# Transposing k and q on VectorE, norms from a diagonal, and a rebuilt join in a fused delta-rule and mixer kernel

## The chip, the cores and the metric

The kernel runs on one core of a Trainium2 chip. The time is device time in microseconds, the median of five runs. TensorE multiplies matrices into PSUM; VectorE and ScalarE do elementwise work; GpSimd ("POOL") sets up constants and issues the weight loads; SyncE ("SP") issues most other transfers. Each engine takes its own instructions strictly in the order of the program. All data is float32.

## The reference, cut to what matters

```python
B, H, S, D = 4, 8, 768, 48
k_n = k / (np.linalg.norm(k, axis=-1, keepdims=True) + 1e-06)
for t in range(S):
    y[:, :, t] = q_t @ state                       # per batch and head, D x D state
    v_old = k_t @ state
    state = state + beta_t * outer(k_t, v_t - v_old)   # k_t is a row of k_n
x = y as (B, S, H * D)                             # d_model = 384
h = x^T @ U @ V                                    # rank 32, over the sequence
u = x + h^T
out = u + relu(u @ w_ch1) @ w_ch2                  # hidden 1536
```

The weights arrive as 64-bit floats and are converted on the chip.

## The kernel before, in words

**Units.** The sequence of each batch is cut into chunks of 64 tokens, 12 a batch; six chunks of all eight heads are a *unit*, so there are eight units, two for each batch. For each unit the kernel needs k and q with the head dimension on the partitions, the products K K^T (`pg`) and K Q^T (`qk`), and the inverse of a triangular 64x64 matrix for each head and chunk (`zt`), which turns the token-by-token recurrence into one step for each chunk.

**Turning k and q (L516 to L535).** k is loaded with tokens on partitions (`kn`), q into `qn`. For each pair of chunks `turn` does four 128x128 transposes on TensorE (`p_t`), and ScalarE copies the result to `kq`. A unit has 24 of them. `products` then forms 16 small products for each pair (`p_g`).

**Norms and c (L443 to L514, L240).** Squares of k, a reduction on VectorE (L464), roots on ScalarE, and, with beta (transposed at the start by `p_bt`, L245), c = beta / norm^2. c changes layout by a transpose `p_ct` (L493) and a round trip through DRAM (`scrc`, `cp`, L499 and L505). v is scaled by the norm (L511).

**Inverse (`blocks`, L602).** `pg`'s 32x32 diagonal blocks go through DRAM (`scr`, L624) to `gs`, where each of 96 partitions holds one block; after a multiplication by c (L652), pairs of VectorE operations (L668, L674) do the substitution in `xt`. The result goes back through DRAM (`scr2`, L683) to `zt` and `zc`. Units 0 and 1 invert 16x16 blocks (15 pairs of operations) and put them together in `join` (L774), a chain of small TensorE products (`p_e`, `p_d`, `p_x`, `p_v`) with evacuations between; it runs in three thirds. Later units invert 32x32 blocks (31 pairs) and need only `p_x` and `p_v` (L722, L736).

**Recurrence (`recur`, L866).** For each chunk: `p_y` from the state, `rhs` (VectorE), `p_s`, `z` (ScalarE), the state's update `p_s` and the output `p_y`, `s` (VectorE). The mixer of a batch follows: `front` (`p_tt`, `p_h`, `p_u`) and `wide` (`p_f` and `p_o`, 36 + 36 matmuls of 128x128x384 for each half of a batch).

**Weights (`load_weights`, L282).** GpSimd loads slices of 768 KB into two alternating buffers (`wide`, `stage`), and five VectorE operations and one ScalarE operation convert each. Parts of w2's place are used early for other tiles (`early`, L218).

**The order.** Nothing is scheduled at run time. Each part is a Python generator; `run` (L140) keeps an estimated clock for each engine and always emits the step that could start first, with a place number as priority. So a changed part moves the order of all engines. On SP every transfer stands in one queue, and of its transfers at most eight are under way: each waits for the one that was issued eight before it. `gate` (L368) makes GpSimd wait for a value before it issues later loads.

## Time and profile before

| | us |
|---|---|
| median of five runs (676.03 to 679.97) | 678.88 |
| profiled execution, its own time | 678.88 |
| its span | 677.1 |
| first p_s of batch 0 starts | 59.81 |
| last p_y of batch 0 starts | 128.81 |
| first p_f starts | 150.34 |

A row of the profile names the line, the engine and the operation, the output and inputs, and the shape. "x8" counts instructions; a float32 matmul counts as two passes, a transpose as one. "Idle before" is the time the engine waited ahead of the instruction and what released it. The span is cut into 40 slices of 16.9 us in the page's second part; its digits are tenths of busy time, and PEclk is the granted TensorE clock in tenths. The busy time by stage gives us of each engine in a stretch of time.

### The profile page before, as it was taken

How to read it: one execution, taken by the hardware profiler on the slowest of the kernel's cores; microseconds unless marked ns; L12 is line 12 of the kernel's file. 1: busy time of each engine (PE TensorE's matmuls, PEld its weight loads, DVE VectorE, ACT ScalarE, POOL GpSimd, SP SyncE). 2: the span in 40 equal slices, each digit the busy share in tenths (PEclk: the TensorE clock that was granted, in tenths of full speed). 3: DMA queues.
4: the chain of work that ended last, by engine and by line, in shares of the span. 5: the costliest groups of instructions: out<-in, count | busy, mean ns of one | idle time of the engine just before them, and what ended most of it. 6: DMA issues, size and time to landing. Idle time of an engine off the chain costs nothing.

```text
span 677.1 us, 19682 instructions
## 1 busy us (share of the span) xinstructions
PE 623.3 (92%) x8676; PEld 399.7 (59%) x8676; DVE 318.1 (47%) x795; ACT 199.1 (29%) x487; POOL 43.3 (6%) x84
## 2 busy tenths in 40 slices
PE   5538799769999999989999999999999999999997
PEld 4437688536555666546556655665655555555554
DVE  6666688578888124871942187368111111000000
ACT  2406456424221352144314422422321221120210
POOL 6451000100100000000000000000000000000000
PEclk9856555759999999999999999999999999999999
DMA  8585747742721332246133321420300000000000
GB/s 123 115 194 151 152 115 188 169 79 35 185 53 37 69 66 60 48 84 122 22 68 64 69 54 45 76 61 2 60 14 26 1 1 24 12 1 23 13 10 24
DMA packets 143892, 46.00 MB, mean 68 GB/s; under 512 B 136960, under 2 KB 140032, under 8 KB 143808
## 3 DMA queue, kind: packets, MB, share of 16 engines
q1 hardware_dynamic: 133952, 30.99, 22.8%
q0 software_dynamic: 3552, 12.88, 6.7%
q10 hardware_dynamic: 6304, 0.89, 0.8%
q8 instruction: 68, 1.11, 0.7%
q14 instruction: 16, 0.13, 0.1%
HBM read 33.62 MB, written 11.11 MB: 66 GB/s over the span
## 4 chain that ended last, share of the span: by engine, by line
PE 81%; DVE 7%; DMA 6%; ACT 2%; SPq 2%; issue 1%; ACTq 1%; DVEq 0%
PE p_o L1058 28%; PE p_f L1038 27%; PE p_y L870 4%; PE p_g L553 3%; PE p_t L529 3%; PE p_s L921 2%; PE p_s L907 2%; DMA scr<-xt 2%; PE p_y L929 2%; DVE xt L674 2%; DVE prod L668 2%; PE p_u L1005 1%; PE p_h L995 1%; PE p_e L794 1%; DMA zt<-scr 1%
## 5 line engine op out<-in xcount | busy, mean ns | idle before, releaser
L1038 PE MATMUL p_f<-ut,w_sb 128*128 128x384 f32 x576 | 204.3, 500 | 0.2 <-ACT h_f L1023 0.2
L1058 PE MATMUL p_o<-w_sb,h_f 128*128 128x384 f32 x576 | 201.1, 495 | 0.0
L1038 PEld LDWEIGHTS p_f<-ut,w_sb 128*128 128x128 f32 x576 | 105.1, 191 | 65.2 <-issue 1.8
L1058 PEld LDWEIGHTS p_o<-w_sb,h_f 128*128 128x128 f32 x576 | 104.6, 190 | 63.4
L1023 ACT ACTIVATE h_f<-p_f 128x384 f32<-128x384 f32 x96 | 47.1, 491 | 205.8 <-PE p_f L1038 205.8
L1028 DVE TENSOR_TENSOR x<-x,p_o 128x384 f32<-128x384 f32 x24 | 13.2, 553 | 130.5 <-PE p_o L1058 130.5
L674 DVE TENSOR_TENSOR xt<-xt,prod 96x112 f32<-96x112 f32 (+21 forms) x216 | 70.5, 326 | 7.4
L668 DVE TENSOR_TENSOR prod<-gs,xt 96x112 f32<-96x112 f32 (+21 forms) x216 | 70.0, 324 | 6.2
L553 PE MATMUL p_g<-kq 48*64 48x64 f32 x1536 | 39.8, 250 | 9.7 <-DVE qk L569 8.2
L944 DVE TENSOR_TENSOR s<-s,p_s 128x192 f32<-128x192 f32 x40 | 14.1, 352 | 69.0 <-PE p_s L921 64.1
L553 PEld LDWEIGHTS p_g<-kq 48*64 48x64 f32 x1536 | 33.4, 159 | 18.6 <-DVE qk L569 7.7
L951 ACT COPY x<-p_y 64x192 f32<-64x192 f32 x96 | 30.0, 313 | 39.2 <-PE p_y L929 34.1
L870 PEld LDWEIGHTS p_y<-s,kq 48*64 48x64 f32 x1408 | 28.4, 149 | 19.6 <-issue 10.9
L535 ACT COPY kq<-p_t 128x512 f32<-128x512 f32 x48 | 27.4, 587 | 38.8 <-PE p_t L529 38.6
L916 ACT COPY z<-p_s 128x192 f32<-128x192 f32 x48 | 15.3, 318 | 73.6 <-PE p_s L907 73.4
L900 DVE TENSOR_TENSOR rhs<-vn,p_y 128x192 f32<-128x192 f32 x44 | 15.5, 351 | 41.2 <-PE p_y L870 40.8
L870 PE MATMUL p_y<-s,kq 48*64 48x48 f32 x1408 | 33.9, 237 | 0.8 <-DVE s L944 0.6
L907 PEld LDWEIGHTS p_s<-rhs,zt 64*64 64x64 f32 x704 | 16.1, 146 | 22.0 <-issue 17.7
L921 PEld LDWEIGHTS p_s<-z,kn 64*64 64x64 f32 x704 | 16.0, 148 | 19.4 <-issue 16.5
L907 PE MATMUL p_s<-rhs,zt 64*64 64x48 f32 x704 | 21.7, 240 | 3.5 <-DVE qk L569 1.7
L794 PE MATMUL p_e<-zt,pg 64*64 64x32 f32 x192 | 12.0, 291 | 13.1 <-DMA zt<-scr 11.9
L637 POOL MEMSET xt<- 96x1056 f32 x6 | 5.9, 978 | 278.8 <-DMA scr<-xt 278.8
(122 smaller groups left out, 530.3 us busy)
## 6 DMA issues: line engine op xcount, KB each, us to landing
wide<-in_moe_w_ch_dram POOLq DMA_DIRECT2D x6, 768.0 KB, 5.3
stage<-in_moe_w_ch_dram POOLq DMA_DIRECT2D x6, 768.0 KB, 5.8
out_dram<-x SPq DMA_DIRECT2D x24, 192.0 KB, 2.1
kn<-in_k_dram SPq DMA_DIRECT2D x60, 72.0 KB, 3.0
qn<-in_q_dram SPq DMA_DIRECT2D x48, 72.0 KB, 3.1
vn<-in_v_dram SPq DMA_DIRECT2D x48, 72.0 KB, 2.5
gs<-scr SPq DMA_DIRECT2D x8, 384.0 KB, 4.0
scr<-xt SPq DMA_DIRECT2D x8, 384.0 KB, 4.5
```

The costliest lines, as they stand in the source:

```text
L529: nc.tensor.transpose(p_t[:, x, j], t[:, c, 2 * j : 2 * j + 2].rearrange("p s d -> p (s d)"), ident,)
L535: nc.scalar.copy(places, p_t)
L553: nc.tensor.matmul(p_g[par][to, c, j], kq[rows, c0 + c, j, 0, cols], kq[rows, c0 + c, j, i, cols], start=True, stop=True,)
L668: nc.vector.tensor_tensor(out=prod, in0=gb[:, :, j : j + 1, j + 1 :].to_broadcast([NP, split, m, w]), in1=xb[:, :, 0:m, j : j + 1].to_broa ...
L674: nc.vector.tensor_tensor(out=xb[:, :, 0:m, j + 1 :], in0=xb[:, :, 0:m, j + 1 :], in1=prod, op=ALU.subtract,)
L870: nc.tensor.matmul(p[half(x ^ par), par, D * (2 * i + j) : D * (2 * i + j) + D], kq[half(par, D), cu, j, i, half(x)], s_old[half(par, D), ...
L907: nc.tensor.matmul(p_s[half(x), par, D * (2 + j) : D * (2 + j) + D], zt[half(x ^ par), cu, par, j], rhs[half(x ^ par), 2 * j + par], start ...
L921: nc.tensor.matmul(p_s[half(par), x, D * j : D * j + D], kn[half(x), cu, 2 * j + par], z[half(x), 2 * j + par], start=True, stop=True,)
L951: nc.scalar.copy(tokens_of(b, c, g), pair_of(p_y, 1)[half(g)])
L1023: nc.scalar.activation(hs[f], p_f, ACTF.Relu)
L1038: nc.tensor.matmul(p_f, w1_sb[:, t, f * 128 : (f + 1) * 128], ut[:, t], start=(t == 0), stop=(t == KT - 1),)
L1058: nc.tensor.matmul(p_os[c], hs[e][:, c * 128 : c * 128 + 128], w2_sb[:, e], start=(e == 0), stop=(e == FT - 1),)
```

## The change

- **k and q, units 2 to 7.** `turn_all` loads them in pieces of 32 tokens by 32 or 16 dimensions straight from DRAM into `qn`, used as a staging tile, with 16 transfers each on SP, and one VectorE transpose of 128x1536 in blocks of 32x32 (L481) writes the turned k or q. `kq` becomes two tiles, `kt` and `qt`. Units 0 and 1 keep TensorE. k is still loaded in its own layout for the recurrence.
- **Norms and c.** The diagonal of K K^T is in `gs` already; its root is the norm. `norm` and c are computed there (four VectorE operations on 96x32), in the layout that the inverse uses; four small matmuls (`p_n`) bring the norm to token layout for v. Beta is loaded in the blocks' layout, four transfers a unit on SP. Squares, reduction, `p_bt`, `p_ct` and c's round trip are gone.
- **Join.** `p_e` and `p_d` work on 32x32 tiles. The blocks for `zt` are no longer loaded but copied from `zc` by ScalarE (`blocks_of_32`), behind `xz`; `zc` is loaded on two queues for unit 0. One VectorE subtraction replaces eight ScalarE and four VectorE pieces.
- **Weights and order.** Odd slices of w2 are staged in w2's own last part; the U and V loads come first on GpSimd; q and v of unit 0 and the first w1 slice wait for unit 0's inverse (`gate(0)`), q and v of unit 1 and later slices for its `zc` (`gate(1)`). Batch 1's recurrence waits for w1's slices, no longer for w2's. The copy of `pg` for units 0 and 1 is shared by ScalarE and VectorE.

In the order that results, SP issues the 16 transfers of unit 2's q ahead of its scr, and on TensorE unit 2's `p_n` stands ahead of batch 0's `p_tt`.

```diff
+    def load_beta(n):
+        b, hf = divmod(n, 2)
+        if n > 1:
+            yield need(("scr", n - 1))
+        yield step(sp=2.1, then=2.5)
+        for i in range(4):
+            g, a = divmod(i, 2)
+            nc.sync.dma_start(
+                out=betas[CS * i : CS * i + CS, n],
+                in_=beta[b, 4 * g : 4 * g + 4, hf * UC * L : (hf + 1) * UC * L].rearrange(
+                    "s (c a t) -> c s a t", c=UC, a=2
+                )[:, :, a],
+            )
...
-            if i % 2:
+            if i in (W2 + 1, W2 + 3):
+                at = WIDE * (2 + (i - W2 + 1) // 2)
+                wide = early[:, at : at + 2 * n].bitcast(I32)
...
-                yield need(("weights", i - 2), *[("v", 0)] * (i == 1), *[("opened", 1)] * (i == 2))
+                last = i - 2 if i < W2 + 5 else i - 1
+                yield need(("weights", last))
+                if i > 1:
+                    yield need(("opened", i > 3))
...
+    def turn_all(n):
+        b, hf = divmod(n, 2)
+        stage = qn.rearrange("p c s d -> p (c s d)")
+        places = stage.rearrange("p (x j m d) -> p x j m d", x=2, j=2, d=BK)
+        yield need(("queries turned", n - 1))
+        for i, (name, src) in enumerate((("keys", k), ("queries", q))):
+            for par in range(2):
+                for half_d in range(2):
+                    rows = slice(L * par + BK * half_d, L * par + BK * half_d + BK)
+                    ds = slice(BK * half_d, min(D, BK * half_d + BK))
+                    for x in range(2):
+                        yield step(sp=1.2)
+                        for j in range(2):
+                            h = 4 * (x ^ par) + 2 * j + par
+                            nc.sync.dma_start(
+                                out=places[rows, x, j, :, 0 : ds.stop - ds.start],
+                                in_=src[b, h, hf * UC * L : (hf + 1) * UC * L, ds].rearrange(
+                                    "(m t) d -> t m d", t=BK
+                                ),
+                            )
+            emitted((name, n), 8.0)
+            yield need((name, n), ("room", n))
+            yield step(dve=1.8)
+            nc.vector.transpose(made[n][0][i].rearrange("p x j c t -> p (x j c t)"), stage)
+            emitted((name + " turned", n), 0.1)
...
         def key_pair(c0):
-            yield from turn([(kn, c0), (kn, c0 + 1)], kq[:, c0 : c0 + 2, :, 0])
+            if n < 2:
+                yield from turn([(kn, c0), (kn, c0 + 1)], kq[0][:, :, :, c0 : c0 + 2])
             yield from products(c0, 0)
...
-        yield need(("c", n), ("inverted", n - 1))
+        yield need(("inverted", n - 1), ("beta", n))
+        norm = small.tile([NP, BK], FP32, name="norm")
+        yield step(act=0.25, then=0.1)
+        nc.scalar.sqrt(norm, gs.rearrange("p i j -> p (i j)")[:, 0 : BK * BK : BK + 1])
+        yield step(dve=0.9, then=0.1)
+        nc.vector.tensor_scalar_add(norm, norm, 1e-6)
+        cp = small.tile([NP, BK], FP32, name="cp")
+        nc.vector.reciprocal(cp, norm)
+        cb = small.tile([NP, BK], FP32, name="cb")
+        nc.vector.tensor_tensor(out=cb, in0=cp, in1=betas[:, n], op=ALU.mult)
+        nc.vector.tensor_tensor(out=cp, in0=cp, in1=cb, op=ALU.mult)
+        def norms():
+            yield step(pe=0.25, then=0.1, take=("one",))
+            p_n = ps_one([128, CS], "p_n")
+            for i in range(4):
+                nc.tensor.matmul(
+                    p_n[BK * i : BK * i + BK], norm, ident[0:NP, CS * i : CS * i + CS],
+                    start=True, stop=True,
+                )
...
-            nc.sync.dma_start(out=zc[BK * i : BK * i + BK], in_=blk[i])
+            two[i % 2].dma_start(out=zc[BK * i : BK * i + BK], in_=blk[i])
...
-        for i in range(4):
-            (nc.scalar if n == 0 else nc.sync).dma_start(out=diagonal(zt, i), in_=blk[i])
...
+                nc.tensor.matmul(
+                    p_e[rows, e], pg[rows, c, j, r, at], zc[rows, e, SB:BK],
+                    start=True, stop=True,
+                )
...
-            nc.scalar.mul(diagonal(zt, i)[0:SB, qs, SB:BK], of, -1.0)
-            if a == 0:
-                nc.vector.tensor_scalar_mul(zc[BK * i : BK * i + SB, :, SB:BK], of, -1.0)
+        nc.vector.tensor_tensor(
+            out=zc[:, :, SB:BK], in0=zc[:, :, SB:BK], in1=p_d, op=ALU.subtract
+        )
+        def blocks_of_32():
+            yield step(act=1.5)
+            for i in range(4):
+                nc.scalar.copy(diagonal(zt, i)[:, qs], zc[quarter[i]])
+            emitted(("diagonal", n, third), 0.1)
```

## The prediction

> **What bounds the kernel now.** I read the page first, then the busy time by stage, then the timelines of TensorE, VectorE and SP, because the page's shares mix two very different stages.
>
> ```profile
> PE 623.3 (92%) x8676; PEld 399.7 (59%) x8676; DVE 318.1 (47%) x795; ACT 199.1 (29%) x487; POOL 43.3 (6%) x84
> PE   5538799769999999989999999999999999999997
> PEclk9856555759999999999999999999999999999999
> ```
>
> From slice 10 on TensorE is full at full clock; before it, TensorE has gaps and is granted about half its clock. The busy time by stage (us; PE, PEld, DVE, ACT and POOL busy, granted clock, DMA share, GB/s) says the same with numbers:
>
> ```profile
> 0.00:40.00 40.00, 22.16 (x346) 18.37 (x346) 27.12 (x72) 11.19 (x27) 23.67 (x56) 0.86 0.75 140
> 60.00:80.00 20.00, 15.05 (x412) 13.14 (x412) 12.94 (x26) 10.69 (x30) 1.12 (x2) 0.59 0.77 177
> 80.00:100.00 20.00, 19.02 (x540) 17.69 (x544) 15.54 (x29) 10.69 (x27) 1.06 (x2) 0.50 0.42 110
> 300.00:400.00 100.00, 99.48 (x1664) 62.07 (x1665) 46.62 (x127) 33.86 (x83) 1.95 (x2) 1.00 0.36 71
> ```
>
> So there are two sums: a chain of latencies up to the first wide product p_f (150.34 us), and a TensorE total from there to 677.1, 526.8 us, in which a TensorE instruction that goes is time that goes. The timeline of TensorE has the points on which the first sum hangs (start, duration, instruction, idle before it):
>
> ```profile
> 47.40 3.59 PE L794 MATMUL p_e<-zt,pg 64*64 64x32 f32 x62 [1.58 <-DMA zt<-scr]
> 59.81 0.75 PE L907 MATMUL p_s<-vn,zt 64*64 64x48 f32 x16
> 70.85 0.39 PE L794 MATMUL p_e<-zt,pg 64*64 64x32 f32 x2 [3.24 <-DMA zt<-scr]
> 116.16 1.92 PE L529 MATMUL p_t<-ident,w_sb 128*128 128x128 f32 x8
> 139.86 1.65 PE L980 MATMUL p_tt<-tt,quarters 128*128 128x384 f32 x2 [5.72 <-DVE tt L977]
> 150.34 4.21 PE L1038 MATMUL p_f<-ut,w_sb 128*128 128x384 f32 x6
> ```
>
> The 5.72 us in front of the second p_tt are VectorE's, which sat behind the blocks of unit 2, as its timeline shows:
>
> ```profile
> 134.73 1.22 DVE L652 TENSOR_TENSOR gs<-gs,cp 96x1024 f32<-96x1024 f32 x1 [6.55 <-DMA gs<-scr]
> ```
>
> **The change, part by part. (a) Up to the inverse of unit 0.** The chain of waits has p_bt (12.40, 2.69 us) between the second and third key product. It goes; the first two pairs' products now stand together, so the third is 9.23 + 2.1 (two products) + 1.05 (p_t) + 0.7 (copy) + 1.1 = 14.2 instead of 16.2, and its evacuation is split over ScalarE and VectorE (0.4): scr leaves at 14.7 instead of 17.01. By the same intervals as before (gs issued 3.8 later, landed 4.0 later by its median) gs is there at 22.5. Before, the multiply at 25.91 waited for cp, the round trip of c through DRAM, which goes. In its place stand, after gs, one small square root (0.2, like L474), four small VectorE operations (0.17+0.30+0.18+0.18, L478 to L483), and a 0.4 us copy of unit 1 that the order puts ahead: 24.1. Gain 1.8. U's and V's conversion stand ahead of these on VectorE; POOL, which no longer issues q first (5.17 us), sends V by about 9 us, so I price that wait at 0; if V were late, the gain here is gone.
>
> **(b) Inverse to first recurrence.** The 30 operations are the same. scr2 takes 5.67 us with vn, V and q in flight; gated, it meets q, a w1 slice and vn, as much: 0 (the bounds are -2.5, as unit 1's scr2 took 3.37, and +1.5). Then zt (4 transfers on ScalarE's queue, last issue 43.26, landed 47.26) goes, and zc's four are split over two queues: 1.1 issue and 4.0 to land instead of 6.4. Gain 1.2. The join, from 47.40 to p_s at 59.81, is 12.4. p_e and p_d become twice as many 32x32 tiles with 16 columns; the nearest row is p_v of L736 (96 passes in 1.02 at full clock, so about 21 ns at half), 64 passes in 1.35 per third against 1.8 and 1.0 before: level. What shortens it is that the eight ScalarE and four VectorE pieces of p_d (0.27 and 0.28 each, taking turns) become one subtraction of 128x128 (0.3) and the transposition (0.43), and that p_x reads zc itself. Step by step: p_e two thirds 2.7, p_d 1.4 after a 0.35 scale, 0.75 on VectorE, p_x 1.0, xz 0.7, four new zt copies of 32x256 (0.37 each, ahead of the last scale on ScalarE) 1.5, zt 0.75, hops: 9.7. Gain 2.7. First p_s: 59.8 - 5.7 = 54.1.
>
> **(c) Recurrence of batch 0, 69.5 us to 129.3.** Unit 1's inverse no longer queues so long behind the joins; its scr2 goes at about 53 (58.68 before) and only zc must land (SP's zt was 2.2 later than zc): of the 4.3 us without work before 71.91 I take 2.3 off. The transposes p_t of unit 2 (1.11+1.92+0.66+0.66+0.65 = 5.0) go: 4.0, as they are only nearly always in the way. VectorE gets two transposes of 128x1536. It does 128x256 in 425 ns and 128x384 in 574, so 1.16 ns a column: about 1.9 us each; one falls ahead of a state update. Against it the reduction (1.35) and four norm operations (0.83) go: 0. [...] The trace grants 0.50 from 80 to 100 us with TensorE 95% busy. [...] I go by the row. Recurrence: 6.3 less, ends near 117.3.
>
> **(d) From there to p_f.** Now SP's queue decides. Behind unit 0's last use (kn goes at 95.70 before, 87.7 now) stand 8 transfers of k (5.8), 8 of v (6.5), **16 of q at 0.55 (8.8)** and only then scr<-pg of unit 2: about 109. Before, gs was issued 7.5 after it and landed 5.4 later: 122 now, 134.64 before. TensorE stands behind it too: p_n (norm of unit 2) is ahead of p_tt. From gs: root 0.3, VectorE 0.95, p_n 0.4, one p_g 0.6 to 1.1, p_tt 2.8, copy 0.6, two p_g 2.2, p_tt 1.65, copy 0.6, then 7.5 as before (8.2 less a p_t and p_g): 17.5, so p_f at 139.5. Of the 12 us won, 10.8 arrive.
>
> **(e) The TensorE-bound rest, 526.8 us.** p_t:
>
> ```profile
> 192.00:300.00 108.00, 4.94 (x32) 1.00 0.28 59
> 300.00:420.00 120.00, 6.01 (x40) 1.00 0.30 61
> 420.00:565.00 145.00, 3.66 (x24) 1.00 0.15 32
> 257.83 1.02 PE p_t L529 x8
> ```
>
> (The first three are p_t's busy time by stage, the last a piece of the chain.) Busy times overlap; the chain has 1.02 for 8, so 96 transposes are 12.2, and 20 of unit 3 after 150 (1.09+1.04+0.66) 2.8. p_n and p_ct (0.29+0.2) give way to four small matmuls (0.3): 1.0 for five units. ScalarE's evacuations (0.59 each) were hidden, nothing. In exchange SP issues 24 more transfers a unit. Their cost is in when they land:
>
> ```profile
> kn<-in_k_dram SPq DMA_DIRECT2D x60, 72.0 KB, 3.0
> zc<-scr SPq DMA_DIRECT2D x24, 48.0 KB, 2.1
> ```
>
> A load of k has 384 pieces of 192 B; the new ones 384 of 128 or 64 B, like zc's. [...] By the rows, though, such a transfer is issued every 0.55 us and lands in 2 to 4, so 16 of them need 12 and a pair of halves with its 1.9 us transposes 28, against some 60 us per unit, with SP's other 24 transfers and waits about 20. By the row the cost is 0. [...] The join of unit 2 is covered too: its inverse starts near 133 and ends near 157, 16 transfers of unit 3's q may stand ahead of its scr2, and its blocks land near 170, while the order brings TensorE to p_x only after 36 p_f, 12 p_o and the products, about 41 us after p_f starts (180). The same 36 p_f (26 us) hide the conversion of w2, staged in w2's own last part: 0, and what a slice is late if that cover is gone. The four beta loads a unit (0.5 each on SP) and the changed order of zt's blocks cost nothing here. What I charge is VectorE's 1.9 us ahead of a rhs or state update: three products of 0.35 us (2.1 with their weights) usually cover it, so 2 in all (bounds -2.5, as TensorE waited twice for the 1.26 us reduction in the chain, and 8 x 1.9 = 15). Sum: 526.8 - 12.2 - 2.8 - 1.0 + 2 = 512.8.
>
> **Sum.** 139.5 + 512.8 = 652.3 of span. The profiled run was 678.88 with a span of 677.1, 1.8 around it, and 678.88 is also the median of the five, so no correction: 654.1.
>
> **Rivals.** (1) The start gains nothing: SP's 16 transfers, or the diagonal's wait for gs, take the place of what went. For it: gs already ended VectorE's longest wait, and (d) leans on an SP order. Against: zt, cp and p_bt are certainly gone. Then 677.1 - 14.0 + 1.8 = 665. (2) Slower: VectorE blocks at the head of its queue. L481 waits for all 16 loads, and behind it stand the rhs and state updates that feed TensorE, which is in order too. Place: units 4 to 7, after 190 us. SP also has outputs in that queue that wait for VectorE (207.5 us of waits on L1028), so loads can start late. With a gain of 25, eight transposes must each be late by 3.1 us beyond their cover for no change; at 5 us each 15 us are lost: 694 at worst, 686 as its middle. Against: DMA share is 0.36 or less there. [...]
>
> **How the numbers follow.** Forecast 0.52 (646 to 661); start gains nothing 0.20 (661 to 673); slower 0.10; more 0.18 (632 to 646). Leaving out a tenth at each end gives 638 to 675. About 0.3% (2 us) is what a measurement of this kernel tells from no change; 677 to 681 is nearly empty between (1) and (2): 0.02. Faster 0.88, slower 0.10.
>
> **What would show it.** Right: scr<-pg of unit 0 near 14.7, first p_s near 54, gs of unit 2 near 122 with p_n and p_tt directly behind it, p_f near 139, p_t at 72 instead of 192, L481 near 1.9 us, and from p_f to the end about 513. Wrong: waits of L481 on qn's loads, gaps on TensorE after 190, or a p_e of unit 1 that still waits 4 us.

## The result, and the profile after

The changed kernel takes 673.74 us (median of 43 runs, 668.24 to 683.01) against 678.97 for the kernel before (80 runs beside it). The ratio is 0.9923, with a 95% interval of 0.9909 to 0.9937: 0.8% shorter, by 5.2 us, and clear of the noise. The ratios leave out runs over 1.5% above the fastest of their kernel; medians do not. The forecast was 654, so the sign was right and a fifth of the gain came. The profiled run took 671.6 us, 2.1 below the median (the one before lies on its median), with a span of 669.9 us (677.1 before). The page of the changed kernel, busy time and the two rows of slices:

```profile
PE 599.5 (89%) x8928; PEld 378.6 (57%) x8928; DVE 324.6 (48%) x788; ACT 172.9 (26%) x430; POOL 42.6 (6%) x82
PE   4268788489969999979999999999999999999997
PEclk9665555589979999989999999989999999999999
```

TensorE is busy 23.8 us less than before (599.5 against 623.3) and the span is only 7.2 us shorter: the gain turned into idle time. TensorE also issues more instructions (8928 pairs against 8676; a pair here is one pass, a weight load and a product, and a float32 matmul is two pairs: the 288 p_f of the program stand as x576 on the page), and the clock row has dips from slice 10 on that were not there before. The busy time by stage (columns as before: stretch, length, PE, PEld, DVE, ACT, POOL busy, granted clock, DMA share, GB/s):

```profile
0.00:40.00 40.00, 16.09 (x276) 12.88 (x276) 23.72 (x69) 9.98 (x23) 18.61 (x47) 0.79 0.73 153
60.00:80.00 20.00, 15.87 (x539) 14.07 (x532) 12.85 (x23) 9.91 (x25) 1.08 (x2) 0.50 0.57 110
80.00:100.00 20.00, 17.27 (x603) 15.45 (x605) 12.97 (x26) 8.42 (x21) 1.06 (x2) 0.50 0.42 121
300.00:400.00 100.00, 99.67 (x1505) 60.40 (x1506) 45.42 (x123) 27.64 (x68) 1.95 (x2) 1.00 0.41 70
```

From 60 to 100 us TensorE is not busier than before (33.1 us against 34.1), but does 1142 passes there instead of 952. The timeline of TensorE at the points on which the first sum hung:

```profile
55.53 0.68 PE L910 MATMUL p_s<-vn,zt 64*64 64x48 f32 x16
126.69 0.68 PE L910 MATMUL p_s<-rhs,zt 64*64 64x48 f32 x16 [0.57 <-DVE rhs L903]
133.80 0.68 PE L932 MATMUL p_y<-z,qk 64*64 64x48 f32 x16 [6.43 <-ACT z L919]
135.73 2.73 PE L974 MATMUL p_tt<-x,u_sb 128*32 128x384 f32 x12
145.75 2.20 PE L1041 MATMUL p_f<-ut,w_sb 128*128 128x384 f32 x6
```

The first p_s is 4.3 us earlier than before (59.81). But from there to the last p_s it takes 71.2 us, where before it took 68.0. Then TensorE waits 6.43 us for ScalarE's copy of z, which stood behind a square root that waited for unit 2's gs (timeline of ScalarE):

```profile
133.15 0.26 ACT L629 ACTIVATE norm<-gs 96x32 f32<-96x32 f32 x1 [6.75 <-DMA gs<-scr]
133.43 0.32 ACT L919 COPY z<-p_s 128x192 f32<-128x192 f32 x1
```

That gs was late on SP, whose timeline has unit 0's betas and unit 2's loads:

```profile
9.26 7.08 SPq L249 DMA_DIRECT2D betas<-in_beta_dram  x8
...
93.48 7.71 SPq L408 DMA_DIRECT2D kn<-in_k_dram  x8
101.56 5.74 SPq L408 DMA_DIRECT2D vn<-in_v_dram  x8
107.40 12.33 SPq L472 DMA_DIRECT2D qn<-in_q_dram  x16
119.83 3.94 SPq L610 DMA_DIRECT2D scr<-pg  x4
129.87 0.32 SPq L621 DMA_DIRECT2D gs<-scr  x1
```

The span cut at four points of the traces shows where the forecast went (us; predicted from the text on record, with step e's 14.0 shared out by where its transposes stood: 20 and 28 in the third part, 68 in the last):

| part | before | predicted | after |
|---|---|---|---|
| start to first p_s | 59.8 | 54.1 | 55.5 |
| first p_s to p_f | 90.5 | 85.4 | 90.2 |
| p_f to p_tt of batch 1 | 141.7 | 135.8 | 143.2 |
| p_tt of batch 1 to the end | 385.1 | 377.0 | 380.9 |
| span | 677.1 | 652.3 | 669.9 |

These are single executions, and the traces of the experiments below show how far such points scatter. In seven traces whose program is the changed kernel's up to the last p_s of batch 0 (its own, root_late, fetch3, pe_turn, less_wide, paced, paced_root's second), the first p_s lies at 55.1 to 57.7 us, the last at 125.6 to 127.6, and the stretch between them is 68.6 to 71.2. In five of these whose program is the same up to p_f, p_f lies at 142.9 to 147.5. In fourteen with the same work behind p_tt of batch 1, that part takes 380.5 to 389.2, with 384.0 as the median, so the 380.9 of the table is a good case. A difference between two traces that is no larger than this shows nothing by itself.

### The profile page after: what moved, and what is told of

It is laid out like the page before. It is cut to its first block, busy times and chain, and to the rows that moved or that the text cites. A ratio compares the mean times of both kernels' runs of the same rounds, so it can differ in the third digit from the quotient of the medians.

```text
span 669.9 us, 20220 instructions
## 1 busy us (share of the span) xinstructions
PE 599.5 (89%) x8928; PEld 378.6 (57%) x8928; DVE 324.6 (48%) x788; ACT 172.9 (26%) x430; POOL 42.6 (6%) x82
## 4 chain that ended last, share of the span: by engine, by line
PE 50%; DVE 1%; ACT 0%; issue 0%
PE p_o L1061 22%; PE p_f L1041 19%; PE p_y L873 2%; PE p_s L910 1%; PE p_s L924 1%; PE p_y L932 1%; PE p_g L538 1%; PE p_v L737 1%; PE p_u L1008 0%; PE p_tt L974 0%; PE p_x L723 0%; PE p_h L998 0%; DVE x L1004 0%; PE p_tt L983 0%; DVE xt L687 0%; DVE prod L681 0%
## 5 line engine op out<-in xcount | busy, mean ns | idle before, releaser
L1061 PE MATMUL p_o<-w_sb,h_f 128*128 128x384 f32 x576 | 205.4, 500 | 1.5 <-DVE w_sb L366 1.5
L1041 PE MATMUL p_f<-ut,w_sb 128*128 128x384 f32 x576 | 200.7, 497 | 0.0
L919 ACT COPY z<-p_s 128x192 f32<-128x192 f32 x48 | 15.3, 318 | 93.6 <-PE p_s L910 93.5
L924 PEld LDWEIGHTS p_s<-z,kn 64*64 64x64 f32 x704 | 16.7, 153 | 23.8 <-issue 21.0
L873 PEld LDWEIGHTS p_y<-s,kt 48*64 48x64 f32 x704 | 17.3, 153 | 22.6 <-issue 13.6
L932 PE MATMUL p_y<-z,qk 64*64 64x48 f32 x768 | 23.2, 240 | 7.0 <-ACT z L919 6.9
L924 PE MATMUL p_s<-z,kn 64*64 64x48 f32 x704 | 22.6, 248 | 5.0 <-issue 3.6
L538 PE MATMUL p_g<-qt,kt 48*64 48x64 f32 x768 | 19.6, 255 | 8.3 <-DVE qk L554 5.2
L873 PE MATMUL p_y<-s,kt 48*64 48x48 f32 x704 | 23.2, 247 | 3.9 <-issue 2.4
L538 PEld LDWEIGHTS p_g<-qt,kt 48*64 48x64 f32 x768 | 16.8, 164 | 13.2 <-issue 9.2
L932 PEld LDWEIGHTS p_y<-z,qk 64*64 64x64 f32 x768 | 18.9, 157 | 8.5 <-ACT z L919 7.2
## 6 DMA issues: line engine op xcount, KB each, us to landing
gs<-scr SPq DMA_DIRECT2D x8, 384.0 KB
scr<-xt SPq DMA_DIRECT2D x8, 384.0 KB
```

Source lines behind the costliest of these rows:

```text
L538: nc.tensor.matmul(p_g[par][to, c, j], kq[0][rows, x, j, c0 + c], kq[i][rows, x, j, c0 + c], start=True, stop=True,)
L873: nc.tensor.matmul(p[half(x ^ par), par, D * (2 * i + j) : D * (2 * i + j) + D], kq[i][half(par, D), x, j, cu], s_old[half(par, D), x, j], ...
L924: nc.tensor.matmul(p_s[half(par), x, D * j : D * j + D], kn[half(x), cu, 2 * j + par], z[half(x), 2 * j + par], start=True, stop=True,)
L932: nc.tensor.matmul(p_y[half(x ^ par), par, D * (2 + j) : D * (2 + j) + D], qk[half(x), cu, par, j], z[half(x), 2 * j + par], start=(c == 0 ...
L1041: nc.tensor.matmul(p_f, w1_sb[:, t, f * 128 : (f + 1) * 128], ut[:, t], start=(t == 0), stop=(t == KT - 1),)
L1061: nc.tensor.matmul(p_os[c], hs[e][:, c * 128 : c * 128 + 128], w2_sb[:, e], start=(e == 0), stop=(e == FT - 1),)
```

## Experiments on the first part: the joins and SP's queue

**The unexplained gaps.** Before the change the profile has next to no gap of TensorE that it puts down to nothing ("issue"), 0.6 us in all (0.3 ahead of a p_t and 0.3 ahead of a p_v). After it there are seven between 48 and 112 us, 10.3 us together:

```profile
48.00 1.31 PE L810 MATMUL p_d<-xe,zn 32*32 32x16 f32 x84 [1.17 <-issue]
51.83 0.91 PE L828 MATMUL p_x<-zc,pg 32*32 32x32 f32 x27 [1.65 <-issue]
75.03 0.47 PE L924 MATMUL p_s<-z,kn 64*64 64x48 f32 x8 [3.58 <-issue]
92.57 0.50 PE L797 MATMUL p_e<-w_sb,pg 32*32 32x16 f32 x19 [1.03 <-issue]
97.10 0.34 PE L873 MATMUL p_y<-s,kt 48*64 48x48 f32 x2 [1.42 <-issue]
101.03 0.29 PE L810 MATMUL p_d<-xe,w_sb 32*32 32x16 f32 x5 [0.49 <-issue]
111.28 0.35 PE L873 MATMUL p_y<-s,kt 48*64 48x48 f32 x3 [0.96 <-issue]
```

They stand in the middle of groups that wait for nobody. The rows between the gap at 75.03 and that at 92.57 add up to 509 passes, between 92.57 and 97.10 to 127, between 97.10 and 101.03 to 127: multiples of 128, with a record missing here and there. The DMA queues have a line that fits. These are that line of the changed kernel, and of two experiments below (half, twice) with fewer and more passes:

```profile
q8 instruction: 70, 1.15, 0.8%
```

```profile
q8 instruction: 67, 1.10, 0.7%
```

```profile
q8 instruction: 76, 1.25, 0.7%
```

Packets and MB: 16.4 KB each. 8928 pairs (x8928 PE and x8928 PEld on the page) at 128 a packet make 69.75, 8544 make 66.75, 9696 make 75.75 (before: 8676 pairs, 67.8, and 68 packets). So a packet is read as a block of 128 pairs of TensorE's program, and the gaps as waits for the next block ("block waits" from here on). Four runs ask what makes them.

*big_pieces*: 32 long pieces a transfer instead of 384 short ones.

```diff
-   out=places[rows, x, j, :, 0 : ds.stop - ds.start],
-   in_=src[b, h, ..., ds].rearrange("(m t) d -> t m d", t=BK),
+   out=flat[rows, x, j, 0 : 2 * UC * (ds.stop - ds.start)],
+   in_=src[b, h, ..., :].rearrange("(t m) d -> t (m d)", t=BK)[:, 0 : 2 * UC * (ds.stop - ds.start)],
```

> Leaves the right keys and queries out: the 32 loads per unit of units 2 to 7 fetch as many bytes from other addresses, in 32 pieces of 1536 or 768 B each instead of 384 pieces of 128 or 64 B; number of transfers, waits and order on every engine are those of the changed kernel. Theory 3 (the many small pieces hold up SP, scr2 and the instruction fetch of TensorE): the gaps on TensorE that the profile ascribes to nothing (10.3 us in all between 54 and 112 us) fall below 3 us, SP's 16 loads take under 9 us instead of 12, the time falls by 8 to 15 us, ratio 0.970 to 0.981. Rival (pieces do not matter, the eight-deep queue and the waits do): ratio 0.989 to 0.993, gaps as before.

Measured: 0.9822 (0.9763 to 0.9882), 670.1 us. The gaps stay, 10.7 us in the same groups, so the pieces do not make them: that half of theory 3 falls. What the pieces cost is on SP: gs of unit 2 is issued 5.2 us after its scr<-pg begins, not 10.0 (6.4 to 10.0 in the seven traces with short pieces), at 123.69 instead of 129.87 (126.1 to 131.4); the two sets of 16 loads take 10.0 and 11.4 us (12.1 and 12.3 in the changed kernel, 10.0 to 12.2 and 11.7 to 14.4 in the seven), so hardly less. p_f comes at 142.0, 3.75 us earlier and 0.9 below the earliest with short pieces. The time is under the changed kernel's by 3.6 us in the medians and 6.9 by the ratios (3 to 11 by its interval), between the two forecasts.

*half* and *twice*: fewer or more passes in the joins, with all else in place. Their expectations and that of join64 count products, and each is two pairs: where they say 192 and 384, it is 384 and 768 pairs, so twice adds 6 blocks, not 3, and the rival's price for it is 12.7 us, not 6.3.

```diff
-        for e, (c, j, r) in enumerate(where):
+        for e, (c, j, r) in list(enumerate(where))[::2]:
...
-                    p_e[rows, e], pg[rows, c, j, r, at], zc[rows, e, SB:BK],
+                    p_e[rows, e : e + 2], pg[rows, c, j, r, at], zc[rows, e : e + 2, SB:BK],
```

(half; p_d alike. twice puts `for _ in range(2):` ahead of either product.)

> Leaves out every second weight load of p_e and p_d in the joins of units 0 and 1: one product takes the columns of two blocks, with the weights of the first, so half of the blocks' values are not the reference's; columns, other work and order are those of the changed kernel, 192 pairs fewer. Theory 5: gaps ascribed to nothing fall from 10.3 to 5 us or less, first p_s 1.5 to 3 us earlier than 55.5, last p_s of the recurrence 4 to 7 us earlier than 126.7. Rival (those gaps come from the DMA traffic at their time): 8 us or more of them stay, last p_s within 3 us of 126.7. In both cases p_f gains less than the recurrence, since gs of unit 2 (133 us) is not moved: ratio 0.986 to 0.993.

> Each p_e and p_d product of the joins of units 0 and 1 is issued twice: 384 more pairs of weight load and product, all other work and its order unchanged. Theory 5 (the gaps that the profile ascribes to nothing are waits for TensorE's next block of program, 256 instructions or 128 such pairs, which come no faster than one in about 3.8 us): 3 more blocks, gaps of this kind at 15 to 22 us instead of 10.3, first p_s 4 to 6 us later than 55.5, last p_s of the recurrence 9 to 12 us later than 126.7. Rival (only the engine's time counts, 16.5 ns a pair at half clock): 6.3 us in all, of them at most 3 before the first p_s, gaps as before.

Measured: half 0.9796 (0.9740 to 0.9852), 665.7 us; twice 1.0164 (1.0103 to 1.0225), 690.1 us. Waits of TensorE that the profile puts down to nothing (us, times, longest), first of half, then of twice:

```profile
PE p_y L874 <- issue: 2.4, 2, 1.4
PE p_d L811 <- issue: 1.7, 1, 1.7
PE p_y L933 <- issue: 0.3, 1, 0.3
```

```profile
PE p_d L812 <- issue: 6.5, 5, 2.0
PE p_e L798 <- issue: 6.1, 5, 1.8
PE p_x L830 <- issue: 3.4, 1, 3.4
```

4.4 us of gaps with 384 pairs fewer, 19.3 with 768 more. The first p_s is at 53.7 and 64.9 us (55.5), the last at 120.1 and 145.4 (126.7). In twice that is 24 ns for each pair put in, against 16.5 ns of engine time: 12.7 us of engine time and 9.0 of added gaps make 21.7, and 18.7 were measured. In half next to no engine time goes, as the columns stay. Two rows of the changed kernel compare 64 passes of 16 columns with 32 of 32:

```profile
54.42 1.18 PE L797 MATMUL p_e<-zc,pg 32*32 32x16 f32 x64 [0.86 <-ACT zt L849]
56.13 1.06 PE L845 MATMUL p_v<-xz,zn 32*32 32x32 f32 x32
```

Twelve such groups would be 1.4 us shorter (an estimate from these rows); 5.9 us of gaps went too, and the last p_s came 6.6 us earlier. So in these runs the number of instructions cost, not only the engine's time: theory 5 holds. Forecast for twice were 9 to 12 us, from the count of products; for the doubled count the 18.7 are in line. In less_wide, gaps at 48.48, 52.03 and 55.90 us end 3.55 and 3.87 us apart, in the changed kernel 48.00 and 51.83 are 3.83 apart: in these traces a block came no faster than that, while 127 passes of p_e on 32x32 tiles took 2.10 us (changed kernel, 44.26).

What half won also arrived, against its forecast that gs would not move: unit 2's kn was asked for at 87.33 us instead of 93.48, gs issued at 120.26 instead of 129.87, p_f came at 137.05 (8.7 earlier), p_tt of batch 1 at 280.03 (8.9 earlier), and the median is 8.1 us lower.

*join64* undoes the 32x32 joins of units 0 and 1: p_e, p_d and the rest of the join are those of the kernel before.

```diff
+        for i in range(4):
+            (nc.scalar if n == 0 else nc.sync).dma_start(out=diagonal(zt, i), in_=blk[i])
...
-            for i, rows in enumerate(quarter):
+            for g in range(2):
                 nc.tensor.matmul(
-                    p_e[rows, e], pg[rows, c, j, r, at], zc[rows, e, SB:BK],
+                    p_e[half(g), e], pg[half(g), c, j, r],
+                    zt[half(g), c, j, r].rearrange("p (a t) -> p a t", a=2)[:, :, SB:BK],
```

> Undoes one part alone: the joins of units 0 and 1 on 64x64 tiles as before (p_e and p_d in 16 products a third instead of 32, zt's diagonal blocks by four more transfers a unit, p_d's pieces back through ScalarE and VectorE, two columns of the mask); all else is the changed kernel. Theory 5 (the 192 added pairs cost far more than their engine time, as they bring TensorE to the next block of its program too soon): gaps ascribed to nothing at 5 us or less instead of 10.3, the recurrence from first to last p_s 63 to 67 us instead of 71.2, last p_s 2 to 5 us earlier than 126.7 although the first p_s is 1 to 3 us later than 55.5; time 3 to 7 us under the changed kernel, ratio to the kernel before 0.982 to 0.988. Rival (step b was right that the 32x32 joins save 2.7 us and zt 1.2, and they cost nothing after that): first p_s near 59, last p_s 3 to 4 us later than 126.7, ratio 0.996 to 1.000.

Measured: 0.9943 (0.9919 to 0.9967). First p_s at 61.26 us, last at 124.81: 63.6 us between them instead of 71.2, with 1.1 us of gaps (4.4 in the whole trace). So the new join is worth 5.7 us up to the first p_s (4 to 6 by the seven traces) and gives 7.6 back by the last one (5 to 8). The mechanism is theory 5's, but the 1.9 us that are left do not arrive, and the forecast of 3 to 7 us is missed: kn of unit 2 is asked for no earlier (94.72 us), gs is issued at 130.50, about where the changed kernel has it, and p_f comes at 147.04.

*mixjoin_root* takes the short join for unit 0, where TensorE waits for it, and the old one for unit 1.

```diff
-            begin(join(n, third, pg, zt, zc, zn), ...)
+            begin((join if n == 0 else join64)(n, third, pg, zt, zc, zn), ...)
```

> Unit 0 joined on 32x32 tiles as in the changed kernel, unit 1 on 64x64 tiles as before (four more transfers of zt for unit 1), unit 2's square root behind the recurrence on ScalarE. Theory 5 (the short join is worth having where TensorE waits for it, and the extra pairs cost block waits where it does not): first p_s at 55 to 56 us as in the changed kernel, first to last p_s 63 to 67 us as with 64x64 joins, so the last p_s at 119 to 122 instead of 126.7 and p_f at 136 to 141; 4 to 8 us under the changed kernel, ratio to the kernel before 0.980 to 0.987. Rival (both ends are given back by the next late thing, SP's gs of unit 2 and the end of batch 1): ratio 0.988 to 0.993.

Measured: 0.9995 (0.9967 to 1.0024). The recurrence is as expected (first p_s 56.8, last 122.5, 65.7 us between), the time is not: p_f at 144.1, behind a 5.2 us wait for the norm of unit 2. And new waits for blocks have appeared, 3.08 us at 185.72 in p_x and 1.60 at 190.56 in p_v, bursts of 96 passes in which the changed kernel's trace has no such wait. So the bursts that wait are not the same in the two traces, and the pairs that stand ahead of them are not either.

**The square root and SP's order.**

```diff
+        if n == 2:
+            yield need(("rec", 1))
         norm = small.tile([NP, BK], FP32, name="norm")
```

> Theory 1 (ScalarE blocks the recurrence): the square root of unit 2's diagonal stands ahead of the last z copy on ScalarE and waits for gs until 133.1 us, so the last p_y is 6.4 us late. With the root behind the recurrence, the last p_y comes at about 128 instead of 133.8, p_tt at about 129, and p_f 3 to 6 us earlier than 145.8: time 1 to 6 us under the changed kernel's 673.7, ratio to the kernel before 0.984 to 0.991. Rival (the late gs itself decides, whichever instruction waits for it): VectorE's four norm operations wait for the same gs ahead of the copy of tt, so p_f stays at 145 to 146 and the ratio at 0.992.

*root_late*: 0.9873 (0.9827 to 0.9918), 672.0 us. The last p_y came at 126.74, 7 us earlier, and p_f at 147.62, no earlier (142.9 to 147.5 without the edit): the rival's mechanism, as VectorE's norm operations wait for the same gs ahead of the copy of tt (second p_tt at 137.77). The second p_tt is 1.7 us earlier than in the changed kernel, but TensorE's rows are longer from there: this p_tt takes 1.63 us against 0.91, the first p_h 1.66 against 0.92 (the changed kernel is granted 0.72 from 126 to 148 us). ScalarE's 6.4 us were a shadow of gs, and theory 1 falls for p_f. The 3 us that the ratio is under the changed kernel's (0 to 7 by its interval) are not explained by p_f.

*root_late_scr_first* adds, in the loads of unit 2's queries, a need that is met once gs<-scr of the unit stands on SP:

```diff
+            if i == 1 and n == 2:
+                yield need(("asked", n))
```

> As the run before, and on SP the 16 loads of unit 2's queries stand behind its scr<-pg and its gs instead of ahead of them. Theory 2 (SP's order is the missing term of step d): scr<-pg leaves at about 108 instead of 119.8, gs lands 10 to 12 us earlier, near 122, and p_f comes at 135 to 138 instead of 145.8: ratio 0.977 to 0.982. Rival (the recurrence itself ends near 128 and is what decides once gs is early): p_f at 140 to 142, ratio 0.985 to 0.988.

Measured: gs issued at 123.07 (6.8 us earlier), p_f at 139.86 (5.9 earlier), and a ratio of 0.9997 (0.9966 to 1.0027). So gs did set p_f, but not by as much as theory 2 had it (scr<-pg left at 115.8, as its products on TensorE come no earlier). Part of this is no gain at all: 96 passes of p_g (2.3 us in the changed kernel), which stood ahead of p_f, stand behind it here. The rest, and more, was lost later: 102.6 us from the first p_s to p_tt of batch 1, against 94.7, with 96 passes more of p_g in that stage.

*join64_root*, join64 with the root moved in the same way, shows it from the other side.

> join64, and unit 2's square root behind the recurrence on ScalarE. If ScalarE's wait still ends last there (6.4 us before the last p_y in the changed kernel), 1 to 4 us under join64. Rival (gs decides all the same, as in the run that moved the root alone): within 1.5 us of join64.

Measured: 0.9939 (0.9914 to 0.9965), the same as join64: the rival, by the time. In its trace p_f came at 140.25 us all the same, and the stage behind took 99.3 us; from 282 us to its end 16 passes of p_y take 0.64 to 0.68 us there, against 0.41 to 0.45 from 197 to 278.

## Experiments on the second part: batch 1 and what follows

**Was a transpose worth its time?** *pe_turn* gives units 4 to 7 their transposes on TensorE back.

```diff
+        if n > 3:
+            yield from fetch(n, "q", qn[:, :, :, 0:D], q, (0, 0))
+            return
...
-            if n < 2:
+            if n not in (2, 3):
                 yield from turn([(kn, c0), (kn, c0 + 1)], ...)
```

> Units 4 to 7 transpose their keys and queries on TensorE again (96 transposes, evacuated by ScalarE), and load q in 8 transfers in place of 32 split loads of k and q a unit; everything else is the changed kernel. Theory (step e: p_t was worth 12.2 us and the added loads and transposes on VectorE cost 2): 8 to 12 us slower than the changed kernel, ratio to the kernel before 1.004 to 1.010. Rival (what p_t gave was taken back by the loads and by VectorE's waits): within 3 us of the changed kernel, ratio 0.990 to 0.997.

Measured: 1.0063 (1.0030 to 1.0095), 0.0140 or 9.5 us above the changed kernel. Step e had 12.2 less 2, so this part of the change does what was forecast, with its DMAs priced at 0. But 8.0 us of the difference lie after p_tt of batch 1 (388.9 us against 380.9, for 72 transposes, 9.2 us by step e's price; the mean clock of the profiled run is 0.899 here and 0.906 there) and only 1.2 between the first p_s and p_tt of batch 1, for 24 of them, 3.1 us by the same price.

**The stage that does not pass time on.** In the changed kernel TensorE waits 4.67 us at 188.53, and VectorE ahead of it for zc, whose transfers stood on SP behind 16 loads of unit 3's queries. TensorE and then VectorE:

```profile
188.53 1.13 PE L538 MATMUL p_g<-qt,kt 48*64 48x64 f32 x32 [4.67 <-DVE qk L554]
```

```profile
186.30 0.58 DVE L778 STREAM_TRANSPOSE zn<-zc 128x384 f32<-128x384 f32 x1 [5.74 <-DMA zc<-scr]
```

*fetch3* puts those loads behind zc of unit 2:

```diff
+            if i == 1 and n == 3:
+                yield need(("fetched", 2))
```

> On SP the 16 loads of unit 3's queries stand behind scr2, zt and zc of unit 2 instead of ahead of them. Theory 4 (VectorE's transposition zn waits at the head of its queue for zc, and p_g waits behind it on TensorE): the 4.67 us gap of TensorE at 188 us and the 5.7 us of VectorE ahead of it go, the first p_s of batch 1 comes 3 to 5 us earlier than 194.3. If the time won arrives, the ratio to the kernel before is 0.985 to 0.988. Rival (the 144 wide products of batch 0 run out before batch 1's recurrence ends, so that end decides and hands nothing on): p_tt of batch 1 stays within 1.5 us of 289, ratio 0.990 to 0.993.

Measured: 0.9934 (0.9897 to 0.9971). The gap is gone and the first p_s of batch 1 comes at 187.26 (7.0 earlier; 2.8 of them are p_f's, and 96 passes of p_g, 2.3 us in the changed kernel, now stand behind it), and p_tt of batch 1 at 288.37 instead of 288.97. Theory 4 named the cause of the wait, and its removal is worth nothing: the rival. Instead TensorE waits 2.98 us for a slice of w2 (1.52 before), 1.92 for kt (0.43) and more at the end.

*less_wide* takes TensorE's work out of the same stage.

```diff
-            for f in range(0, FT, 3):
+            ft = FT - 3 if (b, i) == (0, 1) else FT
+            for f in range(0, ft, 3):
```

> Leaves out 9 of the 144 wide products of batch 0 (the last three of twelve terms of each of three output blocks), 6.3 us of TensorE's time in the stage between the first p_s and the p_tt of batch 1, where the changed kernel spends 94.7 us. Step e counted a TensorE instruction that goes as time that goes: 94.7 falls to about 88.4. Theory 6 (in this stage the recurrence's own chain ends it: with the wide products used up one chunk earlier, one more chunk runs bare, at half clock): the stage falls by 2 to 4.5 us only, to 90 to 93.

Measured: the stage takes 92.3 us instead of 94.7, 2.4 less for 6.3 us of work, as theory 6 has it (94.5 to 97.2 in five other traces with the same work there). The kernel before took 94.5 us for this stage: TensorE's busy time fell by 3.2 us (93.6 to 90.4), the stage did not. The whole kernel is at 0.9912 (0.9874 to 0.9950), not to be told from the changed kernel's 0.9923.

*paced* spreads the same wide products over the recurrence:

```diff
-            yield need(w1_there(f))
+            yield need(w1_there(f), pace(f))
```

(p_o alike; `pace` asks of group g that chunk (g - 17) / 2.55 - 1 of batch 1 is through.)

> The changed kernel, with the wide products of batch 0 held back during batch 1's recurrence (a group of three waits until as many chunks as 2.55 groups each are through), so that the last of them stand in the last chunk instead of ending 1.3 chunks before it; nothing else is changed. Theory 6 (the bare end and the lower clock behind it cost time): the stage from the first p_s to p_tt of batch 1 falls from 94.7 us to 90 to 93, granted clock 1.0 from 280 to 310 us instead of 0.92 and 0.91, 2 to 5 us under the changed kernel, ratio to the kernel before 0.985 to 0.990. Rival (the gaps only move to where the products were taken from): within 1.5 us of the changed kernel, 0.990 to 0.995.

> root_late_scr_first (root behind the recurrence, unit 2's query loads behind its scr<-pg and gs; p_f came at 139.9 there, 5.9 us earlier than in the changed kernel, yet the time was 0.9997 of the kernel before, with 2.3 bare chunks at the end of batch 1) with the wide products held back as in paced. Theory 6: the stage from first p_s to p_tt of batch 1 falls from 102.6 us to 92 to 96, and the early start now arrives: ratio 0.980 to 0.987. Rival (the order on SP or VectorE took it back, not the bare end): stage above 98, ratio 0.993 to 1.000.

Measured: paced 0.9900 (0.9869 to 0.9931), 670.4 us, its stage 93.6 us. This is 1.1 us off the stage, less than expected, and the lower clock behind it did not go. Granted clock is the third figure from the right, first of the changed kernel, then of paced:

```profile
280.00:290.00 10.00, 7.60 (x193) 4.80 (x193) 9.42 (x27) 1.89 (x6) 0.00 (x0) 0.92 0.21 45
290.00:300.00 10.00, 8.02 (x127) 4.05 (x121) 8.86 (x19) 3.18 (x9) 0.00 (x0) 0.91 0.48 92
```

```profile
280.00:290.00 10.00, 7.65 (x164) 4.39 (x166) 9.55 (x21) 1.02 (x4) 0.00 (x0) 1.00 0.22 51
290.00:300.00 10.00, 9.56 (x119) 5.22 (x112) 6.26 (x16) 3.38 (x9) 0.00 (x0) 0.53 0.52 99
```

So "the bare end causes the dip" falls (the bare end is the last chunks, with no wide products left beside them); the kernel before had 1.00 here with TensorE busy 7.68 us of 290 to 300. paced_root_first: 0.9974 (0.9942 to 1.0006), stage 99.1 us, the rival. Its early p_f (142.4) was already used up at the first p_s of batch 1 (194.2), with a 3.28 us wait for a block on the way. Here too 96 passes of p_g have moved from ahead of p_f to behind it. In half an earlier gs and p_f did arrive, with the same stage of 94.7 us and the order unchanged. So an early start is lost where the order moves work into the stage behind; in join64_root nothing moved, and why its p_f was lost is open.

**Combinations.** *mix_fine* places wide products singly, moves the root and unit 3's loads, and sends the first eight beta loads by GpSimd's queue.

```diff
-            yield step(pe=1.95, take=("mix",))
             for t in range(KT):
+                yield step(pe=0.65, take=() if t else ("mix",))
...
-            nc.sync.dma_start(out=betas[...], ...)
+            (nc.gpsimd if n < 2 else nc.sync).dma_start(out=betas[...], ...)
```

> A combination: the wide products are placed one by one instead of in threes, unit 2's square root stands behind the recurrence, unit 3's query loads behind unit 2's blocks, the eight beta loads of units 0 and 1 go on GpSimd's queue. If the losses that the trace shows (6.4 us at the last z, 4.67 us at 188, 1.8 us at the start, the idle ends of the recurrences with their half clock) were independent, 8 to 12 us under the changed kernel: ratio 0.975 to 0.981. Rival (each is covered by the next late thing: gs at 133 us, then the end of batch 1's recurrence): 0.985 to 0.990.

Measured: 0.9980 (0.9946 to 1.0014), worse than either forecast. p_tt of batch 1 comes 4 us earlier (285.0), and then it takes 390.8 us to the end, not 380.9; in that stretch block waits of 1.80, 1.55, 0.70 and 0.72 us stand in the p_v bursts, where the changed kernel has none. Its start tells what step a missed: scr leaves at 14.42 us, where the changed kernel, with the betas ahead of it on SP, has 16.47. Of these 2.05 us only 0.5 reach the multiplication by c (24.09 against 24.57).

*paced_root* is paced and root_late together.

> paced, and unit 2's square root behind the recurrence on ScalarE. The run with the root moved alone was 1 to 2 us under the changed kernel although its p_f came 1.9 later; so within 2 us of paced: ratio 0.983 to 0.990. Rival (the half clock that TensorE had around p_tt in that run returns): 2 us or more above paced.

> The same kernel as paced_root. If the gains of paced (1 to 3 us under the changed kernel) and of the moved root (1 to 3) add: ratio 0.984 to 0.990. If TensorE's clock comes back earlier with both, as the 660 us runs suggest: 0.976 to 0.983 again.

Measured: 0.9790 (0.9731 to 0.9850), and 0.9843 (0.9796 to 0.9890) in a second measurement: medians 664.5 and 666.6 us. Both intervals lie below that of the changed kernel, so this version beats both kernels. The trace of the second run has p_f at 144.2 us and p_tt of batch 1 at 284.7, 1.5 and 4.3 us earlier than the changed kernel. The sum of the two edits' own gains would be 0.985, so nothing more than adding is shown.

## Why the prediction was right in sign and wrong in size

- **(a) Right but for one queue.** Forecast: scr at 14.7 us, the multiplication at 24.1. It was 16.47 and 24.57, since the first eight beta loads held SP from 9.26 to 16.34. The step did not count them at all (step e called beta loads free). 1.3 us were won instead of 1.8.
- **(b) Mechanism right, one cost missed.** scr2 took 7.0 us to land, near the bound of +1.5 and not the 0 that was taken, so zc was asked for at 40.94 as before (40.96). zt's wait went. The join took 11.3 us instead of 9.7; the two block waits in it are 2.8. First p_s 55.5, not 54.1.
- **(c) Here the first part failed.** The step "64 passes in 1.35 per third against 1.8 and 1.0 before: level" (of b) priced twice as many tiles by their engine time alone. That time was no worse than forecast (64 passes in 1.05 to 1.18 us), but the program that brings them was priced at nothing: 127 such passes took 2.10 us, and where TensorE waited for the next block it came 3.55 to 3.9 us after the last. The recurrence was to take 63.2 us to its last p_y, which is 61.8 to its last p_s by the distance of the two before (1.4), and took 71.2 (68.6 at least in the seven traces; 68.0 before the change); the block waits in it are 7.5. half, twice and join64 show this cost by removing it, doubling it and undoing it: with the old joins the same stretch took 63.6, and half, with as many pairs as the old joins, was 8 us faster in all than the changed kernel. Waits of TensorE that the profile puts down to nothing were 0.6 us before and 10.3 with the bursts of 32x32 tiles.
- **The clock in (c).** I went by the granted 0.50. Both clocks were seen, with the same program. In root_late, whose mean clock over the span is 0.936 (0.906 in the changed kernel), 16 passes of p_y take 0.40 and 0.41 us at 81.11 and 84.04, where the changed kernel has 0.64; at 87.60 stands a block wait of 1.59 us that the changed kernel does not have, and the p_y at the chunk ahead of the last comes only 1.1 us before the changed kernel's (123.07 against 124.20). In less_wide the granted clock is 1.00 in each stretch from 50 to 90 us, but 32 passes of p_g take 1.10 us at 81.92, as at the granted 0.50, and 0.79 only at 87.76. One burst, first of the changed kernel (clock 0.50 from 80 to 100 us), then of less_wide (1.00 from 80 to 90, 0.57 from 90 to 100):

```profile
90.72 0.82 PE L797 MATMUL p_e<-w_sb,pg 32*32 32x16 f32 x45
```

```profile
90.46 0.56 PE L797 MATMUL p_e<-w_sb,pg 32*32 32x16 f32 x45
92.76 0.50 PE L797 MATMUL p_e<-w_sb,pg 32*32 32x16 f32 x19 [1.75 <-issue]
```

The burst goes on at 92.76 us after a wait of 1.75, at 92.57 after 1.03 in the changed kernel. less_wide's last p_s comes 0.8 us before the changed kernel's (125.87 against 126.69). So the rows were shorter, the block wait behind them was longer, and about 1 us was left by the end of this stage, no more than such points scatter (125.6 to 127.6).
- **(d) Right in what decides, wrong in its sizes.** SP's queue set gs and gs set p_f. kn went at 93.5 (87.7 forecast, from step c), the 8 loads of k held SP 8.1 us (5.8), those of v 5.8 (6.5), the 16 of q 12.4 (8.8), scr to gs 10.0 (7.5), and gs was there 3.3 later (5.4): 133.2 against 122. From gs it took 12.6 us to p_f, not 17.5, as TensorE's clock was 1.0 from 140 us on. The step checked VectorE's and TensorE's queues and not ScalarE's, but that wait cost no p_f (root_late).
- **(e) Here the second part failed.** The sentence "a TensorE instruction that goes is time that goes" holds after p_tt of batch 1 (8.0 us for 72 transposes in pe_turn), and not between p_f and there: 143.2 us instead of 135.8. The working took busy time in a stage from 192 to 300 us as proof, while in it the recurrence's chain is what ends last (2.4 us for 6.3 in less_wide; 94.5 us before and 94.7 after for the stage from the first p_s). TensorE's idle time in this part rose from 2.4 to 10.4 us. "The join of unit 2 is covered too" was wrong by its times (blocks at 186, not 170), but fetch3 shows that this cost nothing.
- **(e), after p_tt of batch 1: a clock that was taken as full.** Here 3.9 us are missing in this trace, and 7.0 in the median of the fourteen. The step took the full clock of the row from 300 to 400 us for all of it. The trace has dips of the clock at 290 to 300 us (0.91) and 430 to 450 (0.93 and 0.90) that before does not have. For nine traces with the same work there is a clock by stretches of 10 us over this part, and all nine have such a dip within 20 us of p_tt. With a mean clock of 0.99 this part took 380.9 to 384.7 us (changed kernel, twice, paced_root_first, less_wide), with 0.98 385.0 to 385.7 (paced_root, paced, fetch3), with 0.97 389.2 (mixjoin_root), and half, between 0.97 and 0.98, took 384.0; before, 1.00 and 385.1, with its transposes. So in these nine, on the whole, the longer this part, the lower its clock; that the dips cost what is missing is argued from this, no run removes them, and what sets them off is open.
- **Signs.** L481 took 1.78 us (1.9). Sixteen short loads took 10.0 to 14.4 us, near the 12 that the row gave. And TensorE's p_t after the change are 48: the list said 72, a slip, as the sums counted the six units that lost them (144 of 192).
- **Rivals.** Rival 2's place was nearly right (a stall at the head of VectorE's queue, behind a transfer), but the instruction was zn and not L481, for whose loads VectorE waits 1.2 us in all. Rival 1 (665 us) had the nearer time for the wrong reason: the start gained 4.3 us before the first p_s, and lost it after. No run shows what the range of 632 to 646 would need: with 1.00 granted from 50 to 90 us, in less_wide, the last p_s came 0.8 us earlier.

## What to carry to other kernels

Count instructions, not only engine time: where a stage's TensorE works on small tiles, divide its pairs of weight load and product by 128 and ask whether each block lasts longer than the 3.55 to 3.9 us in which the next one came here; "issue" gaps in the middle of a group, multiples of 128 apart, were the sign here. And before an instruction that goes is counted as time, ask of each stage what ends last in it: take a known amount of work out and see how much of it arrives. A stall that is seen in the trace need not be on the path: three of those found here (6.4, 4.7 and 2.0 us) were removed, and p_f, p_tt of batch 1 and the inverse of unit 0 hardly moved.

## What the runs showed of the hardware that was not expected

- TensorE's program came in packets that fit 128 pairs each (70, 67 and 76 packets for 8928, 8544 and 9696 pairs), no closer than 3.55 to 3.9 us apart where they were waited for, and a burst of 32x32 tiles outran them (127 passes of p_e in 2.10 us).
- The number of pieces of a transfer hardly changed how long sixteen of them held SP (10.0 to 14.4 us with 384 pieces each, 10.0 and 11.4 with 32 and the same bytes); from scr<-pg to gs behind them it took 6.4 to 10.0 us and 5.2.
- A wait of TensorE of 1.83 us (paced, 289.80) was followed by a granted clock of 0.53 from 290 to 300 us and 0.79 from 300 to 310, with TensorE busy 9.56 and 9.69 of 10 us; one of 1.08 us (changed kernel, 300.04) by 1.00 from 300 to 310.
